# A recurrent attention and two expert layers on one core: masks moved to the Gram eviction, weights split by bit fields, r expanded on the host, another order of the instructions

## The chip, the cores and the metric

The kernel runs on one core of a Trainium2 chip. Time is the device time of one launch in microseconds (us); less is better. The core has TensorE (PE, matrix products), VectorE (DVE), ScalarE (ACT), GpSimd (POOL) and SyncE (SP), which here issues all the transfers. Each engine works through its own list of instructions in the order in which the program gives them, and an instruction waits until the semaphores that it names are set; so whatever stands behind a waiting instruction on the same engine waits too.

## The reference

Three parts follow each other. The first is a recurrence over 768 steps for 4 x 8 heads of width 40; the other two work on 3072 tokens of width 320.

```
for t in range(768):                       # state: 40x40 per head
    y[t]  = r[t] @ state
    Sa    = state @ a[t]
    state = state*w[t] - outer(Sa, b[t]) + outer(v[t], k[t])
x = y as (3072, 320)
xn = x / rms(x) * g;  x = (silu(xn@w_gate) * (xn@w_val)) @ w_out       # 64-bit weights, inner width 1536
logits = x@gate;  P = 8 rounds of row and column normalization of exp(logits)
out = sum over 8 experts of P[:,e] * (relu(x@w1[e]) @ w2[e])           # inner width 1024
```

## The kernel before, in words

**The recurrence** is cut into 24 chunks of 32 steps (c = 0 to 23), and the eight heads into three groups (s = 0, 1, 2 with 3, 3 and 2 heads). `early(c,s)` has what doesn't need the state: it loads a, b, k, v, w (`ldE`) and r (`ldr`), makes running products of w (`scan`, `rec`), scales a, b, k by them (`ag`, `bb`, `kk`), spreads r and scaled a over a block diagonal with three ACT instructions each (`rb`, `abe`), multiplies the Gram matrices on PE (`gr`) and evicts them to the tile W (`Wg`). W goes to DRAM (`stL`) and comes back in another layout, once for a batch of chunks as the input of a triangular inverse (`ldL`, `subst`), and once for each chunk and group as the tile V (`ldW`). `subst` inverts by 31 steps of a product (`mul`, L383) and a subtraction (`sub`, L384) on DVE. Its result returns through DRAM as `th`. `late2` makes from V the block diagonal `lak`, a masked copy in V (`vm`) and `kb`. `chain(c,s)` then carries the state: `Sb` (block diagonal of the state), c1 (transpose), c2, c3, c4 (with the inverse `th`), c5, the new state F and its decayed form Rn for the next chunk, and y, which is stored. So one chunk's chain starts from the chunk before it; a batch's chains wait for that batch's inverse.

**The first expert layer (moe1)** works in six blocks j of 512 tokens, and a block needs y of four chunks. `xload`, `xprep` and `xsplit` load, normalize and split x into two parts; then 12 steps f per block follow, each with two `up` groups of 8 matmuls (L596; `sig`, `sgm`, `pr`, `h`, `l` evict them) and one `down` group of 8 (L612 to L618). Its weights come as 64-bit floats. `decode(f,k)` splits each of 48 pieces into two 32-bit parts with ACT, DVE and POOL instructions (`da` to `dl`, L522 to L531) and stores them in DRAM, from where each f loads them. The three working tiles a, p, q have one buffer each, so a piece begins when the piece before has left them.

**The second layer (moe2)** runs 8 experts x 6 blocks x 8 steps: 8 matmuls up, 12 down (L712, L725 to L727). The kernel also inspects w against limits (`wx`, `wmin`, `wmax`) for a fallback path.

**The order** is not written by hand. Every piece of work is given to a planner (`Plan`) with an engine, a duration, a due time, and what it reads and writes. `order` runs a list schedule over these: on each engine, of what is ready it takes what is due first. The result is the fixed list of each engine. Due times of chunk c come from `tm` (T00, 21 us a chunk at first, then TSL = 29); decoding is due from DEC0 in steps of DECT; what is not marked `fix` takes its due time from what needs it. Until the first `up`, matmuls on zeros (`fill`, L308) are put where the plan leaves PE idle.

Of the kernel before, what the change touches and what calls it, by code (L numbers as in the profile page):

```python
# [31 lines left out]
VW=2*X2+X2  # L32
# [18 lines left out]
def host_attn(r,k,v,w,a,b,nch=NC):  # L51
# [52 lines left out]
class Plan:  # L104
# [3 lines left out]

    LAT={("ACT","PE"):.267,("P","PE"):.25,("P","ACT"):.23,("PE","ACT"):.25,("DVE","P"):.23,("PE","DVE"):.25,("ACT","DVE"):.16,
# [3 lines left out]
    def add(self,eng,dur,due,fn,reads=(),writes=(),after=(),tail=0.0,take=None,give=None,label="",fix=False,cols=None,x=None):  # L113
        self.ops.append(dict(cols=dur*2270 if cols is None else cols,eng=eng,dur=dur,due=due,fn=fn,reads=list(reads),writes=list(writes),after=list(after),
            tail=1.5+(x or 0) if eng=="SP" and x else tail,x=x,take=take,give=give,label=label,fix=fix,id=len(self.ops)))
    def lat(self,a,b): return self.LAT.get((a["eng"],b["eng"]),.2)
    def order(self,slots,free,slack=1.4,slack_sp=2.0):
# [39 lines left out]
        evq=sorted([0.0]+list(free.values()))  # L157
        while len(res)<n:
            while fut and fut[0][0]<=now+1e-9:
                r,i=heapq.heappop(fut); soon[ops[i]["eng"]].discard((r,ops[i]["due"],i)); heapq.heappush(pend[ops[i]["eng"]],(ops[i]["due"],i))  # L160
            for e,h in pend.items():
                while h and free.get(e,0.0)<=now+1e-9:
                    skipped=[]; pick=None
                    while h:
                        d,i=heapq.heappop(h)
                        t=ops[i]["take"]
                        if t and (not ring[t] or min(ring[t])[0]>now+1e-9):
                            skipped.append((d,i)); continue
# [10 lines left out]
                    end=now+o["dur"]; free[e]=end; tail=o["tail"]  # L179
                    if e=="SP" and o["x"]:  # L180
# [71 lines left out]
def attention(G_,I,xT,scrL,scrT,nch,tm,T=21):  # L252
# [66 lines left out]
    def early(c,s,due):  # L319
# [4 lines left out]
        o=spot("W",0,c)[0]; plan.place(("W",s,c),o+VW*H0[s],o+VW*(H0[s]+q))  # L324
# [23 lines left out]
        if 'A'[c%len('A')]=="D": A("DVE",dve(3*q*C),due,lambda: nc.vector.tensor_copy(*wg()),["gr"],["W"],s,c,give=("gr",s,c),label=f"Wg{c},{s}")  # L348
        else: A("ACT",act(3*q*C),due,lambda: nc.scalar.activation(out=wg()[0],in_=wg()[1],func=ACTF.Copy),["gr"],["W"],s,c,give=("gr",s,c),label=f"Wg{c},{s}")
# [12 lines left out]
    def subst(k,due,span):  # L362
# [8 lines left out]
        o=spot("TT",0,k)[0]; parts=[(0 if y=="D" else 1,a,e) for y,a,e in [["D",0,C]]]  # L371
# [3 lines left out]
        for y,(z,a,e) in enumerate(parts):  # L375
            eng,cost=(("DVE",dve),("P",pool))[z]; tn=f"tmp{y}"
            for j in range(a,C-1):
# [5 lines left out]
                A(eng,cost(r*m),dd,lambda j=j,sh=sh,t=t,V=V,x=tt[:,a:a+r]: V.tensor_tensor(t,x[:,:,j:j+1].to_broadcast(sh),lu[:,j:j+1,j+1:].to_broadcast(sh),ALU.mult),[("TT",y,k),("LU",0,k)],[kt],label=f"mul{'.abc'[y]}{k},{j}")  # L383
                A(eng,cost(r*m),dd,lambda j=j,t=t,V=V,x=tt[:,a:a+r]: V.tensor_tensor(x[:,:,j+1:],x[:,:,j+1:],t,ALU.subtract),[kt],[("TT",y,k)],label=f"sub{'.abc'[y]}{k},{j}")  # L384
# [10 lines left out]
    def late2(c,s,due):  # L395
        m=KT[s]; q=NH[s]; k=bof[c]; c0,nb=batches[k]; n=KE[s]
        V=X["V",s,c]; Vm=V[:m]
        if c>0:
# [13 lines left out]
        A("ACT",z(s,3*act(8*D),.64),due,expand,["V",("cst",)],["kb"],s,c,label=f"kb{c},{s}")  # L412
# [5 lines left out]
    def chain(c,s,due):  # L418
# [510 lines left out]
```

## Time and profile before

| | |
|---|---|
| time, median of 3 runs | 2495.6 us (2489.71 to 2497.9) |
| profiled execution: time; span from the first to the last instruction | 2487.21 us; 2485.4 us |
| busy PE; DVE; ACT; POOL | 2387.0; 1099.4; 876.6; 651.5 us |
| granted clock of TensorE, mean | 0.975 |
| HBM read; written | 183.01; 45.61 MB |
| matmuls on zeros (L308) | 1051, 138.0 us |

Busy time is the time in which at least one instruction of the engine was under way. Ends of matmuls are modelled, so a busy PE is not PE at its peak. The profile's "idle before" of an instruction is the time in which its engine stood still just before it, with what ended that.

### The profile page before, as it was taken

What the parts mean: (1) busy time and instruction counts of PE and PEld (TensorE: products, weight loads), DVE (VectorE), ACT (ScalarE), POOL (GpSimd) and SP (SyncE); (2) the same over time, 40 slices, a digit from 0 to 9 for tenths busy, and PEclk for the clock granted to TensorE, in tenths of its full rate; (3) what the DMA queues carried; (4) which work ended last, traced back from release to release, by engine and by line L of the source; (5) the groups of instructions that cost most, each with busy time, mean ns of one, the idle gap of its engine ahead of it and who ended that gap; (6) DMA issues with size and microseconds to landing.
All of it is one profiled execution on the core that took longest, in us unless ns stands there. A gap on an engine that the chain in (4) does not pass through costs nothing.

```text
span 2485.4 us, 43767 instructions
## 1 busy us (share of the span) xinstructions
PE 2387.0 (96%) x17435; PEld 2057.2 (83%) x17435; DVE 1099.4 (44%) x2169; ACT 876.6 (35%) x2079; POOL 651.5 (26%) x803
## 2 busy tenths in 40 slices
PE   8889889998999999799999999999999999999998
PEld 6777667787777877589899999988999989999887
DVE  7897996757576433621252222222222222222222
ACT  6465647565574544332221211211211211211111
POOL 5465655444453344330041100200200200100000
PEclk9998899999999999899999999999999999999999
DMA  9677678685876657740010000100100100000000
GB/s 241 185 184 159 172 208 229 163 221 152 205 192 176 177 143 215 229 126 1 11 37 1 27 21 1 46 2 1 47 1 1 47 1 10 27 1 1 11 25 31
DMA packets 263663, 231.59 MB, mean 93 GB/s; under 512 B 131801, under 2 KB 225049, under 8 KB 263449
## 3 DMA queue, kind: packets, MB, share of 16 engines
q1 hardware_dynamic: 263448, 228.70, 33.9%
q8 instruction: 139, 2.28, 0.4%
q14 instruction: 76, 0.61, 0.1%
HBM read 183.01 MB, written 45.61 MB: 92 GB/s over the span
## 4 chain that ended last, share of the span: by engine, by line
PE 74%; DVE 9%; DMA 3%; issue 1%; ACT 1%; SPq 0%; POOL 0%; DVEq 0%; ACTq 0%; POOLq 0%
PE bank L712 29%; PE bank L725 9%; PE bank L726 9%; PE bank L727 9%; PE bank L596 7%; DVE f L383 3%; DVE f L384 2%; PE bank L612 1%; PE bank L444 1%; PE bank L443 1%; PE bank L450 1%; PE bank L615 1%; PE bank L463 1%; PE bank L616 1%; PE bank L462 1%
## 5 line engine op out<-in xcount | busy, mean ns | idle before, releaser
L712 PE MATMUL bank<-r,r 128*128 128x512 f32 x3072 | 774.3, 394 | 0.0
L717 DVE SCALAR_TENSOR_TENSOR r<-bank,r 128x512 fp32r<-128x512 f32 x384 | 265.2, 691 | 893.6 <-ACT r L716 893.5
L712 PEld LDWEIGHTS bank<-r,r 128*128 128x128 f32 x3072 | 561.4, 188 | 101.5
L716 ACT ACTIVATE r<-bank 128x512 fp32r<-128x512 f32 x384 | 229.8, 599 | 1054.3 <-PE bank L712 1054.3
L725 PE MATMUL bank<-r,r 128*128 128x320 f32 x1536 | 475.4, 310 | 0.0
L726 PE MATMUL bank<-r,r 128*128 128x320 f32 x1536 | 474.2, 309 | 0.0
L727 PE MATMUL bank<-r,r 128*128 128x320 f32 x1536 | 474.1, 309 | 0.0
L705 POOL TENSOR_TENSOR r<-f,r 128x320 fp32r<-128x320 f32 (+1 forms) x128 | 120.9, 949 | 904.4 <-ACT r L704 901.9
L596 PE MATMUL bank<-r,r 128*128 128x512 f32 x1152 | 311.3, 416 | 11.7 <-ACT r L585 4.9
L726 PEld LDWEIGHTS bank<-r,r 128*128 128x128 f32 x1536 | 288.3, 188 | 17.2
L725 PEld LDWEIGHTS bank<-r,r 128*128 128x128 f32 x1536 | 288.3, 188 | 16.7 <-issue 1.0
L727 PEld LDWEIGHTS bank<-r,r 128*128 128x128 f32 x1536 | 288.3, 188 | 0.0
L596 PEld LDWEIGHTS bank<-r,r 128*128 128x128 f32 x1152 | 217.1, 196 | 62.6 <-ACT r L585 6.0
L312 ACT ACTIVATE f<-f,f 120x128 f32<-120x128 f32 (+1 forms) x568 | 183.1, 393 | 16.4 <-POOL f L337 9.5
L308 PE MATMUL bank<-f 128*128 128x256 bf16 x1051 | 138.0, 290 | 1.5 <-POOL f L298 1.5
L735 DVE SCALAR_TENSOR_TENSOR f<-bank,f,f 128x320 f32<-128x320 f32 x168 | 84.3, 544 | 112.6 <-PE bank L727 112.6
L308 PEld LDWEIGHTS <-f 128*128 128x128 bf16 x1051 | 106.7, 103 | 20.7 <-POOL f L298 1.5
L605 POOL TENSOR_TENSOR r<-f,r 128x512 fp32r<-128x512 f32 x72 | 93.7, 1301 | 109.6 <-ACT r L603 107.3
L383 DVE TENSOR_TENSOR f<-f,f 96x60 f32<-96x60 f32 (+27 forms) x248 | 113.9, 459 | 15.8 <-DMA f<-sL 11.0
L384 DVE TENSOR_TENSOR f<-f,f 96x60 f32<-96x60 f32 (+27 forms) x248 | 112.1, 452 | 4.6
L315 POOL TENSOR_TENSOR f<-f,f 120x480 f32<-120x480 f32 (+1 forms) x69 | 71.2, 1032 | 151.7 <-DVE f L470 132.0
L443 PE MATMUL bank<-f,f 96*96 96x72 f32 (+1 forms) x576 | 95.9, 251 | 2.6 <-DVE f L471 1.3
(156 smaller groups left out, 2775.1 us busy)
## 6 DMA issues: line engine op xcount, KB each, us to landing
r<-wd SPq DMA_DIRECT2D x72, 768.0 KB, 4.8
r<-wd SPq DMA_DIRECT2D x72, 320.0 KB, 3.6
sL<-f SPq DMA_DIRECT2D x96, 176.0 KB, 4.1
f<-in_pk SPq DMA_DIRECT2D x48, 301.9 KB, 4.8
wd<-r SPq DMA_DIRECT2D x48, 256.0 KB, 3.4
f<-in_w SPq DMA_DIRECT2D x64, 192.0 KB, 2.4
f<-sL SPq DMA_DIRECT2D x48, 216.0 KB, 4.3
f<-in_w SPq DMA_DIRECT2D x64, 160.0 KB, 2.3
```

What stands on the lines that cost most here:

```text
L308: def fill(): nc.tensor.matmul(G_.banks[0][:,0:256],fz[:,0:128],fz[:,128:384],start=True,stop=True)
L312: nc.scalar.activation(out=out[:,:,q,:],in_=plain,func=ACTF.Copy,scale=mbe[:KE[s],q:q+1])
L383: A(eng,cost(r*m),dd,lambda j=j,sh=sh,t=t,V=V,x=tt[:,a:a+r]: V.tensor_tensor(t,x[:,:,j:j+1].to_broadcast(sh),lu[:,j:j+1,j+1:].to_broadcast ...
L384: A(eng,cost(r*m),dd,lambda j=j,t=t,V=V,x=tt[:,a:a+r]: V.tensor_tensor(x[:,:,j+1:],x[:,:,j+1:],t,ALU.subtract),[kt],[("TT",y,k)],label=f"s ...
L596: for i,(a,k) in enumerate(PAS): PE.matmul(b,w[:,k//3,3*g+k%3],xs[:,a],start=i==0,stop=i==7)
L705: A("P",pool(n),0,lambda lo=lo,hi=hi,raw=raw: PO.tensor_tensor(lo,raw,hi,ALU.subtract),[kr,kh],[kl],label=f"wl{e},{f},{z}")
L712: for i,(a,k) in enumerate(PAS): PE.matmul(b,w[:,k],t[:,a],start=i==0,stop=i==7)
L716: A("ACT",act(TB),due+1.8,lambda: AC.activation(out=h,in_=bk[ku],func=ACTF.Relu),[ku],[kh],fix=True,label=f"R{e},{j},{f}")
L717: A("DVE",dve(TB),due+2.4,lambda: DV.scalar_tensor_tensor(l,bk[ku],0.0,h,ALU.max,ALU.subtract),[ku,kh],[kl],give=ku,fix=True,label=f"Q{e}, ...
L725: PE.matmul(p,h[:,s],w[:,0],start=f==0,stop=False)
L726: PE.matmul(p,h[:,s],w[:,1],start=False,stop=False)
L727: PE.matmul(p,l[:,s],w[:,0],start=False,stop=f==7)
```

## The change

1. The Gram matrices are masked (strictly upper triangle) when they are evicted: `Wg` is a DVE product of PSUM with the mask instead of an ACT copy. So `vm` goes, V is narrower (VW = 2*X2+D), and `lak` is three ACT copies with a scale instead of one POOL product.
2. `ag`, `bb`, `kk` go from POOL to DVE; `Sb` goes from POOL to ACT (three scaled copies).
3. r spread over the block diagonal is made on the host and loaded (`ldrb`, one transfer for each c and s, three buffers), so the ACT work `rb` goes.
4. F is written by one DVE instruction over both parts instead of two (F, Fy). In c3 of the two-head group the four products with `lak` come first, then the four with `abl`; before they alternated.
5. `decode`: the clamp of small weights (`da`, `db`) is left to the fallback. The high part is cut out of the high word by masks, the low part is put together as an integer, converted by ACT (`dg`) and multiplied by the exponent on POOL (`dl`). Per piece DVE has dc, dd, di, dq, ds (five, before six), ACT dh and dg (two, as before), POOL one (before two). `dc` and `di` now read the high words of the 64-bit pieces directly (every second word).
6. moe2 inspects the 64-bit weights too: 60 more loads, each with two DVE instructions.
7. The planner treats POOL and those DVE instructions that are marked `port` as one resource. Batches of the inverse are 1, 3, 3, 3, 3, 3, 4, 4 chunks (before 2, 3, 3, 3, 3, 3, 3, 4), and the first batch's inverse is two independent parts. Due times change (T00, DEC0, DECT, MINC; `lo` keeps decoding from becoming due earlier than its step).

```
-VW=2*X2+X2
+VW=2*X2+D
+WW=3*X2
-    for n in [2, 3, 3, 3, 3, 3, 3, 4]:
+    for n in [1, 3, 3, 3, 3, 3, 4, 4]:
...
-                        if t and (not ring[t] or min(ring[t])[0]>now+1e-9):
+                        if t and (not ring[t] or min(ring[t])[0]>now+1e-9) or ops[i]["port"] and port>now+1e-9:
...
+                    if o["port"]: port=end
...
-        rb=q5(tl("rb",n,s,c)[:,0:LP*q],q); r=X["r",s,c]
-        A("ACT",z(s,.88,.59),due,lambda: bd_act(rb,r,s),[("r",0,c),("cst",)],["rb"],s,c,label=f"rb{c},{s}")
+        rbt=tl("rb",n,s,c)[:,0:LP*q]; rb=q5(rbt,q)
+        A("SP",.5,due-T,lambda: nc.sync.dma_start(out=rbt,in_=I[f"rb{s}"][:,c]),[],["rb"],s,c,x=n*LP*q*4/360e3,label=f"ldrb{c},{s}")
-        A("P",.42,due,lambda: nc.gpsimd.tensor_tensor(ag,x(0),G4[:,:,0:C],ALU.mult),["pk","G"],["ag"],s,c,label=f"ag{c},{s}")
+        A("DVE",.2,due,lambda: nc.vector.tensor_tensor(ag,x(0),G4[:,:,0:C],ALU.mult),["pk","G"],["ag"],s,c,port=True,label=f"ag{c},{s}")
...
-        else: A("ACT",act(3*q*C),due,lambda: nc.scalar.activation(out=wg()[0],in_=wg()[1],func=ACTF.Copy),["gr"],["W"],s,c,give=("gr",s,c),label=f"Wg{c},{s}")
+        A("DVE",dve(3*q*C),due,lambda: nc.vector.tensor_tensor(*wg(),mji.unsqueeze(1).unsqueeze(1).to_broadcast([128,q,3,C]),ALU.mult),["gr",("cst",)],["W"],s,c,give=("gr",s,c),label=f"Wg{c},{s}")
...
-        A("P",z(s,.95,.68),due,lambda: nc.gpsimd.tensor_tensor(lak,Vm[:,:,D:X2].unsqueeze(2).to_broadcast([m,4,q,C]),
-            mla[:m,:q].unsqueeze(1).to_broadcast([m,4,q,C]),ALU.mult),["V",("cst",)],["lak"],s,c,label=f"lak{c},{s}")
+        def lakf():
+            for x in range(q): nc.scalar.activation(out=lak[:,:,x,:],in_=Vm[:,:,D:X2],func=ACTF.Copy,scale=mbt[:m,x:x+1])
+        A("ACT",z(s,.88,.59),due,lakf,["V",("cst",)],["lak"],s,c,label=f"lak{c},{s}")
...
-            Z("P",z(s,.95,.68),0,lambda: bd_tt(Sb,Rx[:,:,C:],s,D),["Rx"],["Sb"],"Sb")
+            Z("ACT",z(s,.98,.66),0,lambda: bd_act(Sb,Rx[:,:,C:],s),["Rx"],["Sb"],"Sb")
...
+            else:
+                for g in range(4): l(g,start=g==0,stop=False)
+                for g in range(4): h(g,start=False,stop=g==3)
...
-        A("ACT",act(n),due,lambda: AC.activation(out=Fl(a),in_=Fl(hi),func=ACTF.Abs),[kr],[ka],label="da"+z)
-        A("DVE",dv2(n),due,lambda: DV.tensor_scalar(Fl(a),Fl(a),2.0**-15,None,ALU.max),[],[ka],label="db"+z)
-        A("P",pool(n),due,lambda: PO.tensor_tensor(Fl(q),Fl(q),Fl(a),ALU.subtract),[ka],[kq],label="de"+z)
-        A("P",pool(n),due,lambda: PO.tensor_tensor(Fl(p),Fl(p),h,ALU.subtract),[kh],[kp],label="df"+z)
-        A("DVE",dve(n),due,lambda: DV.scalar_tensor_tensor(l,Fl(q),2.0**-20,Fl(p),ALU.mult,ALU.add),[kq,kp],[kl],label="dl"+z)
+        A("DVE",dv2(n),due,lambda: DV.tensor_scalar(a,src1,3,0x3ffff000,ALU.logical_shift_left,ALU.bitwise_and),[kr,ks1],[ka],port=True,lo=due,label="dc"+z)
+        A("DVE",dv2(n),due,lambda: DV.tensor_scalar(a,hi,0x1ff,15,ALU.bitwise_and,ALU.logical_shift_left),[kr],[ka],port=True,lo=due,label="di"+z)
+        A("DVE",dve(n),due,lambda: DV.scalar_tensor_tensor(q,lo,17,a,ALU.logical_shift_right,ALU.bitwise_or),[kr,ka],[kq],port=True,lo=due,label="dq"+z)
+        A("ACT",act(n),due,lambda: AC.activation(out=Fl(a),in_=q,func=ACTF.Copy,scale=2.0**-35),[kq],[ka],lo=due,label="dg"+z)
+        A("DVE",dv2(n),due,lambda: DV.tensor_scalar(p,p,-0x800000,None,ALU.bitwise_and),[kh],[kp],port=True,lo=due,label="ds"+z)
+        A("P",pool(n),due,lambda: PO.tensor_tensor(l,Fl(a),Fl(p),ALU.mult),[ka,kp],[kl],lo=due,label="dl"+z)
...
-        t=max(t,tm(4*j+4)+MLAG); dt=max(U,(tm(4*j+8)-tm(4*j+4))/12 if j<NB-1 else U)
+        t=max(t,tm(4*j+4)+MLAG+MINC*j); dt=max(U,(tm(4*j+8)-tm(4*j+4))/12 if j<NB-1 else U)
...
-DEC0,DECT=20.0,4.6; MLAG=30.0
+DEC0,DECT=-60.0,4.0; MLAG,MINC=30.0,6.0
...
-T00,TSL=70.0,29.0
+T00,TSL=55.0,29.0
```

DVE's list at the start of the program, before: one decoding piece (L523 to L531), then running products and reciprocals (L335, L336). Names like f_640_202 are areas of one big SBUF arena.

```order
L523 TENSOR_SCALAR f_320_203<-f_320_203 128x256
L524 TENSOR_SCALAR f_320_203<-f_320_203 128x256
L525 SCALAR_TENSOR_TENSOR f_320_204<-f_640_202,f_320_203 128x256
L527 TENSOR_SCALAR f_320_203<-f_320_204 128x256
L528 SCALAR_TENSOR_TENSOR f_320_205<-f_640_202,f_320_203 128x256
L335 SCALAR_TENSOR_TENSOR f_132_97<-f_644_96,f_132_89 120x132
L336 RECIPROCAL f_128_98<-f_132_97 120x128
```

The same place after the change (L343 is `scan`, L344 `rec`, L345 to L347 `ag`, `bb`, `kk`, L537 to L543 decoding, L356 `Wg`):

```order
L343 SCALAR_TENSOR_TENSOR f_132_97<-f_644_96,f_132_89 120x132
L344 RECIPROCAL f_128_98<-f_132_97 120x128
L345 TENSOR_TENSOR f_128_99<-f_644_96,f_132_97 120x128
L343 SCALAR_TENSOR_TENSOR f_132_107<-f_644_106,f_132_89 120x132
L346 TENSOR_TENSOR f_128_100<-f_644_96,f_128_98 120x128
L347 TENSOR_TENSOR f_128_101<-f_644_96,f_128_98 120x128
L537 TENSOR_SCALAR f_320_205<-f_640_204 128x256
L343 SCALAR_TENSOR_TENSOR f_132_115<-f_644_114,f_132_89 80x132
L538 SCALAR_TENSOR_TENSOR f_320_206<-f_640_204,f_320_205 128x256
L345 TENSOR_TENSOR f_128_109<-f_644_106,f_132_107 120x128
```

The first chunk's products now stand ahead of the first decoding piece, and products that POOL made are between them.

PE's list at c3 of the two-head group, before (one of 23 places; L443 is the product with `lak`, L444 that with `abl`; two of the four pairs):

```order
L443 MATMUL bank_86<-f_864_143,f_384_151 64x72
L444 MATMUL bank_86<-f_288_190,f_384_176 64x72
L443 MATMUL bank_86<-f_864_143,f_384_151 64x72
L444 MATMUL bank_86<-f_288_190,f_384_176 64x72
```

After (L448 and L449 are the same products):

```order
L448 MATMUL bank_83<-f_736_149,f_384_157 64x72 x4
L449 MATMUL bank_83<-f_288_177,f_384_174 64x72 x4
```

The eight products are the same; the change of operand shape between 64 and 80 rows happens once instead of seven times.

PE's list behind the recurrence's last c5 (L460), before: the rest of moe1's block 4 begins.

```order
L460 MATMUL bank_86<-f_864_154,f_320_164 80x72 x4
L612 MATMUL bank_79<-r_512_226,r_640_222 128x512
...
L617 MATMUL bank_81<-r_512_225,r_640_222 64x512
L596 MATMUL bank_85<-r_2560_197,r_1536_218 128x512 x8
L596 MATMUL bank_83<-r_2560_197,r_1536_218 128x512 x8
L612 MATMUL bank_79<-r_512_217,r_640_227 128x512
```

After (L472 is c5, L609 `up`, L625 to L630 `down`):

```order
L472 MATMUL bank_83<-f_736_156,f_320_166 80x72 x4
L609 MATMUL bank_85<-r_2560_199,r_1536_220 128x512 x8
L625 MATMUL bank_79<-r_512_219,r_640_224 128x512
...
L630 MATMUL bank_81<-r_512_218,r_640_224 64x512
L609 MATMUL bank_86<-r_2560_199,r_1536_225 128x512 x8
L609 MATMUL bank_84<-r_2560_199,r_1536_225 128x512 x8
```

From the last c5 to the first `up` of block 5, PE's list had 4 `up` groups and 4 `down` groups of block 4; it has 9 and 6 now.

## Rows read from the trace of the kernel before

**Rows 1.** Busy time by stretch of the whole span, chosen as the prediction says
```profile
core 0: us, PE busy (x) PEld busy (x) DVE busy (x) ACT busy (x) POOL busy (x), PEclk, DMA share, GB/s
0.00:397.50 397.50, 346.97 (x3791) 280.17 (x3791) 343.09 (x749) 218.06 (x634) 224.12 (x321) 0.91 0.75 193
397.50:975.00 577.50, 555.53 (x5553) 449.63 (x5553) 332.36 (x703) 323.52 (x849) 248.48 (x309) 0.98 0.68 182
975.00:1016.00 41.00, 22.94 (x94) 16.57 (x92) 22.46 (x30) 23.63 (x42) 28.57 (x25) 0.81 0.83 264
1016.00:1085.00 69.00, 68.68 (x292) 55.23 (x293) 33.75 (x56) 18.97 (x31) 17.60 (x14) 0.97 0.58 189
1085.00:2485.40 1400.40, 1392.91 (x7712) 1255.58 (x7710) 367.78 (x634) 292.42 (x526) 132.73 (x136) 1.00 0.06 19
```
**Rows 2.** Groups of DVE instructions, 0 to 397.5 us: busy us, mean ns | idle before
```profile
L384 DVE TENSOR_TENSOR f<-f,f 96x60 f32<-96x60 f32 (+23 forms) x124 | 59.4, 479 | 1.8
L383 DVE TENSOR_TENSOR f<-f,f 96x60 f32<-96x60 f32 (+23 forms) x124 | 53.3, 430 | 4.7 <-DMA f<-sL 3.1
L523 DVE TENSOR_SCALAR f<-f 128x256 f32<-128x256 f32 (+1 forms) x48 | 30.0, 625 | 13.9 <-ACT f L522 13.4
L531 DVE SCALAR_TENSOR_TENSOR r<-f,f 128x256 fp32r<-128x256 f32 (+1 forms) x48 | 28.0, 583 | 13.0 <-POOL f L530 12.9
L525 DVE SCALAR_TENSOR_TENSOR f<-f,f 128x256 int32<-128x256 int32 (+1 forms) x48 | 25.8, 537 | 3.0 <-DVE r L531 0.5
L524 DVE TENSOR_SCALAR f<-f 128x256 int32<-128x256 int32 (+1 forms) x48 | 22.2, 463 | 1.1
L405 DVE TENSOR_TENSOR f<-f,f 96x128 f32<-96x128 f32 (+1 forms) x14 | 6.5, 467 | 0.0
```
**Rows 3.** Timeline of DVE, first decoding piece, no POOL work beside it: start, us
```profile
4.31 0.29 DVE L524 TENSOR_SCALAR f<-f 128x256 int32<-128x256 int32 x1
4.63 0.43 DVE L525 SCALAR_TENSOR_TENSOR f<-f,f 128x256 int32<-128x256 int32 x1
```
**Rows 4.** Timeline of DVE and POOL, 792 to 800 us
```profile
792.27 0.68 DVE L601 TENSOR_TENSOR f<-bank,f 128x512 f32<-128x512 f32 x1
792.87 0.41 DVE L384 TENSOR_TENSOR f<-f,f 128x252 f32<-128x252 f32 x1
793.20 0.32 DVE L466 TENSOR_TENSOR f<-bank,f 120x160 f32<-120x160 f32 x1
797.98 1.38 DVE L383 TENSOR_TENSOR f<-f,f 128x252 f32<-128x252 f32 x1
799.73 0.28 DVE L405 TENSOR_TENSOR f<-f,f 96x128 f32<-96x128 f32 x1
797.72 1.35 POOL L605 TENSOR_TENSOR r<-f,r 128x512 fp32r<-128x512 f32 x1 [0.52 <-ACT r L603]
```
**Rows 5.** DVE busy with L384 alone, in the inverse of the last batch
```profile
779.20:813.60 34.40, 11.62 (x31) 1.00 0.60 171
```
**Rows 6.** Groups of POOL instructions, 0 to 397.5 us
```profile
L530 POOL TENSOR_TENSOR f<-f,r 128x256 f32<-128x256 f32 (+1 forms) x48 | 39.5, 822 | 43.5 <-ACT r L526 41.7 <-DMA f<-in_wm 1.0 <-DMA sL<-f 0.8
L315 POOL TENSOR_TENSOR f<-f,f 120x480 f32<-120x480 f32 (+1 forms) x23 | 23.2, 1010 | 10.5 <-DVE f L470 9.2 <-DMA f<-in_v 0.7 <-PE bank L443 0.6
L474 POOL TENSOR_TENSOR f<-f,f 120x128 f32<-120x128 f32 (+1 forms) x23 | 13.7, 596 | 0.7 <-POOL f L405 0.7
```
**Rows 7.** Group of the ACT copies onto block diagonals, 0 to 397.5 us
```profile
L312 ACT ACTIVATE f<-f,f 120x128 f32<-120x128 f32 (+1 forms) x270 | 86.6, 393 | 14.1 <-POOL f L337 9.5 <-DMA f<-in_r 3.0 <-PE bank L444 0.9
```
**Rows 8.** Timeline of PE: c3 of a three-head and of the two-head group
```profile
826.63 0.31 PE L443 MATMUL bank<-f,f 96*96 96x72 f32 x2
...
827.93 0.71 PE L612 MATMUL bank<-r,r 128*128 128x512 f32 x2
...
836.85 0.34 PE L443 MATMUL bank<-f,f 64*64 64x72 f32 x2
...
838.99 0.73 PE L612 MATMUL bank<-r,r 128*128 128x512 f32 x2
```
**Rows 9.** Timeline of PE behind the last c5, and at block 5's first up
```profile
974.94 0.72 PE L460 MATMUL bank<-f,f 128*80 128x72 f32 x8
975.47 0.71 PE L612 MATMUL bank<-r,r 128*128 128x512 f32 x2
...
977.40 3.81 PE L596 MATMUL bank<-r,r 128*128 128x512 f32 x16
981.05 0.62 PE L612 MATMUL bank<-r,r 128*128 128x512 f32 x2
...
1015.80 0.79 PE L596 MATMUL bank<-r,r 128*128 128x512 f32 x1 [1.24 <-ACT r L585]
```
**Rows 10.** Waits of PE, 975 to 1016 us: in total, times, longest
```profile
PE bank L639 <- ACT f L636: 11.2, 1, 11.2
```

More of the change, by code (lines that the diff above doesn't have):

```diff
@@ L56, in host_attn @@
     ins["r"]=np.zeros((120,nch,3,LP),np.float32)
+    for s in range(3):
+        z=np.zeros((NH[s],D,nch,B,NH[s],C),np.float32); e=em(r,s).reshape(NH[s],D,nch,B,C)
+        for q in range(NH[s]): z[q,:,:,:,q]=e[q]
+        ins[f"rb{s}"]=z.reshape(KE[s],nch,LP*NH[s])
     for s in range(3):
@@ L156, in order @@
         now=0.0; res=[]; dma=0.0; dq=[]
-        evq=sorted([0.0]+list(free.values()))
+        evq=sorted([0.0]+list(free.values())); port=0.0
         while len(res)<n:
@@ L465, in chain @@
         c5v=lambda: X["c5",s,c]
-        if c>0: Z("DVE",.235,8.8,lambda: nc.vector.tensor_tensor(F[:,:,0:D],c5v()[:,:,0:D],Rx[:,:,C:],ALU.add),["c5","Rx"],["F"],"F")
-        else: Z("ACT",.23,8.8,lambda: nc.scalar.activation(out=F[:,:,0:D],in_=c5v()[:,:,0:D],func=ACTF.Copy),["c5"],["F"],"F")
+        if c>0: Z("DVE",dve(4*X2),8.8,lambda: nc.vector.tensor_tensor(F,c5v(),Rx,ALU.add),["c5","Rx"],["F"],"F",give=("c5",s,c))
+        else: Z("ACT",act(4*X2),8.8,lambda: nc.scalar.activation(out=F,in_=c5v(),func=ACTF.Copy),["c5"],["F"],"F",give=("c5",s,c))
@@ L468, in chain @@
         if c+1<nch:
             Rn=w4(tl("Rx",n,s,c+1))
[L470 to L472 removed]
+            Z("DVE",.235,9.4,lambda: nc.vector.tensor_tensor(Rn[:,:,C:],F[:,:,C:],G[:,:,C:C+1].to_broadcast([n,4,D]),ALU.mult),["F","G"],[("Rx",s,c+1)],"Rn",port=True)
@@ L529, in decode @@
-        A("P",pool(n),due,lambda: PO.tensor_tensor(Fl(q),Fl(q),Fl(a),ALU.subtract),[ka],[kq],label="de"+z)
-        A("P",pool(n),due,lambda: PO.tensor_tensor(Fl(p),Fl(p),h,ALU.subtract),[kh],[kp],label="df"+z)
-        A("DVE",dve(n),due,lambda: DV.scalar_tensor_tensor(l,Fl(q),2.0**-20,Fl(p),ALU.mult,ALU.add),[kq,kp],[kl],label="dl"+z)
+        if not first:
+            A("ACT",act(n),due,lambda: AC.activation(out=Fl(q),in_=Fl(hi),func=ACTF.Abs),[kr],[kq],lo=due,label="da"+z)
+            A("DVE",dv2(n),due,lambda: DV.tensor_scalar(Fl(q),Fl(q),2.0**-15,None,ALU.max),[],[kq],port=True,lo=due,label="db"+z)
@@ new lines, in decode @@
+        src1,ks1=(hi,kr) if first else (q,kq)
+        A("DVE",dv2(n),due,lambda: DV.tensor_scalar(a,src1,3,0x3ffff000,ALU.logical_shift_left,ALU.bitwise_and),[kr,ks1],[ka],port=True,lo=due,label="dc"+z)
+        A("DVE",dve(n),due,lambda: DV.scalar_tensor_tensor(p,hi,-0x40000000,a,ALU.bitwise_and,ALU.bitwise_or),[kr,ka],[kp],port=True,lo=due,label="dd"+z)
+        A("ACT",act(n),due,lambda: AC.activation(out=h,in_=Fl(p),func=ACTF.Copy),[kp],[kh],lo=due,label="dh"+z)
+        A("DVE",dv2(n),due,lambda: DV.tensor_scalar(a,hi,0x1ff,15,ALU.bitwise_and,ALU.logical_shift_left),[kr],[ka],port=True,lo=due,label="di"+z)
```

96 lines of the change are left out of this document (51 added, 45 removed).

## The prediction

> **What bounds the kernel now.** I read busy time by stretch first [rows 1]. From 1085 us on PE is busy for 1392.9 of 1400.4 us at full clock, and the change leaves its work there as it is. The time is decided before. The stretches are cut at three events. At 397.5 us DVE runs the third group's step behind c4 of chunk 7; by then all 48 decoding pieces and four batches of the inverse are done. At 975 us PE starts the last c5 of the recurrence, and at 1016 us the first `up` of block 5 [rows 9], which had to wait for that c5, the store and load of y and the normalization.
>
> In the first stretch DVE is busy for 343.1 of 397.5 us, PE for 347.0 with many matmuls on zeros among them: DVE sets the pace. In the second PE is busy for 555.5 of 577.5 us: PE sets it, and recurrence and moe1 share it. [...] So there are three terms, one for each stretch.
>
> **First stretch: the balance of DVE.** I compare the work up to the same event, chunk 7's third group behind c4. The new order has there, as the old one, 9 evicted steps of moe1, 24 chain steps and four batches, and 47 pieces begun against 48.
>
> What goes from DVE: the clamp (L523, 30.0 us), the last step of decoding (L531, 28.0) and the masked copies (L405, 6.5): 64.5 us [rows 2]. F and Fy become one instruction, which I count as nothing (it saves one start and adds no columns).
>
> What comes, at durations without POOL beside them: 117 products `ag`, `bb`, `kk` at 0.28, the row of L405 with 128 columns [rows 4], 32.8 us. `di`, 46 at 0.43, 19.8 us, and `dc` 0.14 slower, 47 times, 6.6 us: both now read every second word, the nearest row that does is L525 with 0.43, while the dense L524 takes 0.29 [rows 3]. `Wg`: PSUM rows of 160 and 512 columns take 0.32 and 0.68 [rows 4], so 1.02 ns a column, 0.45 for the 288 columns of a three-head group and 0.35 for 192; 26 and 13 of them are 16.3 us. The split of the first batch adds 54 instructions but no columns; 0.41 us at 252 columns [rows 4] leaves 0.15 without the columns, 8.1 us. Together 83.6; the net is +19 us.
>
> Against that stands what POOL costs DVE. A subtraction of 252 columns takes 0.41 alone, and a product of as many 1.38 beside a POOL instruction of 1.35 [rows 4]. In this stretch L524 takes 463 ns in the mean against 290 alone, L525 537 against 430 [rows 2, 3]; over 48 each that is 8.3 and 5.1 us. The inverse takes 59.4 + 53.3 us [rows 2]; eight times the 11.62 us of a batch with little POOL [rows 5] is 93.0, so 19.7 us. That makes 33 us to get back if POOL were silent. POOL is busy for 224 us there [rows 1]; what stays are one product per piece (39.5), y (13.7) [rows 6] and some 20 us of moe1's small work: a third. So I take two thirds, -22 us, and the busy time ends at -3.
>
> DVE's idle time of 54 us has 13.9 in front of L523, waiting for ACT, and 13.0 in front of L531, waiting for POOL [rows 2]. Both instructions are gone. But the one buffer of each working tile stays: `dc` of the next piece waits for POOL's `dl`, and `ds` for ACT's `dh`. I give half of 26.9 back: -13. **The first term is -16 us.** Its ends: +41, if the products take 0.467 as L405 does in this stretch (+22), nothing of the 33 comes back and the idle time stays; -54, if strided reads cost nothing (-13), all 33 and all 27 come back (19 - 13 - 33 - 27).
>
> [...] No row here shows a one-input DVE instruction that reads with a step; I stay with 0.43.
>
> The chain hides some of this. `Sb` becomes three ACT copies of 0.39 instead of one POOL product of 1.01 [rows 6, 7]: as long, on an engine that is busy for 218 of 397.5 and 323.5 of 577.5 us [rows 1]. ACT loses `rb` and `Wg` and gains `lak` and `Sb`: 8 copies of 0.39 a chunk more, 3.1 us, less three evictions. If ACT were full, 16 chunks of this would be up to 50 us on the chain; with 44% of the second stretch idle on ACT I count nothing. The new loads add 440 KB a chunk to queues that are 0.75 busy in the first stretch and 0.68 in the second; nothing too, unless a Gram product comes to wait for them.
>
> **Second stretch: c3 of the two-head group.** From its first product to what follows it takes 838.99 - 836.85 = 2.14 us; the three-head group's, with as many products and more rows in each, 827.93 - 826.63 = 1.30 [rows 8]. What differs is that 64 and 80 rows alternate. Grouped, seven changes become one; the saving lies between nothing and 0.84 us, and I take 0.8 for the 16 chunks that are left at 397.5 us: **-13 us**.
>
> [...]
>
> **Third stretch: what is left for the gap.** PE's order has 9 `up` and 6 `down` groups of block 4 between the last c5 and block 5, where it had 4 and 4. An `up` group takes 1.83 us (two from 977.40 to 981.05), a `down` 1.93 (975.47 to 977.40) [rows 9]. 5 x 1.83 + 2 x 1.93 = 13.0 us of PE work move from in front of the last c5 into a gap with 18.1 us to spare. The additional evictions stand beside block 5's normalization on ACT and DVE, for which I take 2 us off: **-11 us**.
>
> **moe2.** The weight inspection adds 120 DVE instructions of about half a microsecond, 60 us, beside DVE's 367.8 of 1400.4 [rows 1]. It costs nothing as long as no eviction comes late behind one that waits for its load; such a wait each time, a microsecond, would be 60 us on DVE and still find 900 us idle.
>
> **Sum.** 2487.2 - 16 - 13 - 11 = 2447. The profiled execution was 8.4 us below the median of the runs, so 2455.6; I say **2455 us**. Less than 0.3% (7.5 us) can't be told from no change here.
>
> **The rivals.**
> *DVE stays contended (slower).* The planner's one port is a matter of order; on the chip the two engines still run side by side where no semaphore holds them. If the products run at L405's 0.467 and the inverse at its present 59.4 + 53.3 us, the first term is +41 and eats the other two: 2487 + 41 - 24 = 2504, 2512 as a median. It decides from +24 on. Against it: two thirds of POOL's work is gone from this stretch. 0.15.
> *Same.* The first term ends near +16 to +30 without being that bad, or PE in the second stretch waits for ACT's `Sb` and gives its gains back: 2488 to 2503. 0.11.
> *The start gives nothing.* The net +19 and the relief -22 cancel, the idle time only changes its name: 2487 - 24 = 2463, 2471 as a median, and 2478 if c3 gives half; I count 2468 to 2488. 0.15.
> *The start gives much.* Strided reads are free and decoding no longer stalls DVE: -54 - 24 gives 2409, 2418 as a median; all below 2436. 0.17.
> My forecast, 2436 to 2468, has 0.42.
>
> **How the numbers follow.** Faster holds forecast, a start that gives nothing and one that gives much: 0.74. Same 0.11, slower 0.15. The range leaves out about one in ten at each side: below 2412 and above 2506.
>
> **What would show it.** Right: the third step behind c4 of chunk 7 before 385 us; DVE's busy time to that point within 10 us of 343; subtractions of the inverse nearer to 12 than to 15 us a batch in the first batches; c3 of the two-head group at 1.3 to 1.45 us; PE idle between the last c5 and block 5 under 8 us; span from block 5's first `up` to the end unchanged. Wrong: `ag`, `bb`, `kk` above 0.4 us; DVE waiting for POOL's or ACT's part of decoding as long as now; PE waiting at the Gram products for the host's r, or at c1 for ACT.

## The result and the profile after

The changed kernel takes 2453.5 us in the median of four runs (2447.6 to 2457.55), against 2493.4 for the kernel before on the same chip: a ratio of 0.9837 with an interval of 0.9809 to 0.9865, 1.6% faster. The profiled execution took 2447.6 us with a span of 2445.8, so its span is 39.6 us shorter than that of before.

The windows answer to [rows 1]. The first cut is again the third group's step behind c4 of chunk 7, the second the last matmul of the last c5 (0.4 us behind the cut of [rows 1]; cut like this, before has 577.9 and 40.4 us), the third block 5's first `up`, the fourth 69 us behind it.

```profile
core 0: us, PE busy (x) PEld busy (x) DVE busy (x) ACT busy (x) POOL busy (x), PEclk, DMA share, GB/s
0.00:377.30 377.30, 339.52 (x3865) 281.97 (x3865) 290.62 (x866) 216.15 (x623) 78.25 (x94) 0.91 0.84 216
377.30:932.10 554.80, 528.99 (x5448) 435.24 (x5446) 334.43 (x747) 364.05 (x963) 119.95 (x116) 0.97 0.75 195
932.10:976.80 44.70, 36.55 (x145) 25.57 (x143) 31.36 (x41) 26.97 (x48) 30.83 (x26) 0.89 0.96 310
976.80:1045.80 69.00, 69.00 (x297) 56.11 (x298) 42.37 (x76) 18.52 (x30) 18.99 (x14) 0.97 0.78 246
1045.80:2445.80 1400.00, 1392.19 (x7708) 1254.85 (x7706) 393.62 (x729) 291.87 (x525) 132.68 (x136) 1.00 0.08 25
```

The 39.6 us are divided like this: 20.2 in the first stretch, 23.1 in the second, 4.3 lost again in the third, 0.6 in moe2. In the first, DVE's busy time fell by 52.5 us, but its idle time rose from 54.4 to 86.7. In the second, PE's busy time fell by 27 us and its idle time rose a little. In the third, PE does 14 us more work and idles 8.2 us instead of 18.1.

The groups of DVE up to the first cut answer to [rows 2]; the waits of DVE and of ACT there say what its idle time ended with.

```profile
L391 DVE TENSOR_TENSOR f<-f,f 32x171 f32<-32x171 f32 (+34 forms) x151 | 48.4, 331 | 0.6
L390 DVE TENSOR_TENSOR f<-f,f 32x132 f32<-32x132 f32 (+34 forms) x151 | 47.8, 326 | 2.8 <-DMA f<-sL 2.1
...
L538 DVE SCALAR_TENSOR_TENSOR f<-f,f 128x256 int32<-128x256 int32 (+1 forms) x46 | 20.4, 444 | 0.9
...
L356 DVE TENSOR_TENSOR f<-bank,f 128x288 f32<-128x288 f32 (+1 forms) x39 | 15.3, 408 | 0.8 <-PE bank L353 0.5
L537 DVE TENSOR_SCALAR f<-f 128x256 int32<-128x256 int32 (+1 forms) x47 | 15.1, 320 | 4.3 <-POOL r L544 3.4 <-DMA f<-in_wm 0.8
L540 DVE TENSOR_SCALAR f<-f 128x256 int32<-128x256 int32 (+1 forms) x46 | 14.7, 320 | 1.1
L347 DVE TENSOR_TENSOR f<-f,f 120x128 f32<-120x128 f32 (+1 forms) x39 | 14.6, 376 | 0.0
L543 DVE TENSOR_SCALAR f<-f 128x256 int32<-128x256 int32 (+1 forms) x46 | 13.5, 294 | 37.3 <-ACT r L539 37.0
L345 DVE TENSOR_TENSOR f<-f,f 120x128 f32<-120x128 f32 (+1 forms) x39 | 12.9, 332 | 0.1
L346 DVE TENSOR_TENSOR f<-f,f 120x128 f32<-120x128 f32 (+1 forms) x39 | 12.2, 312 | 0.0
```

```profile
DVE f L543 <- ACT r L539: 37.0, 26, 3.6
...
ACT r L539 <- DMA wd<-r: 35.2, 21, 3.5
```

Read the two waits as one. `ds` (L543) waits 37 us for ACT's `dh` (L539), and `dh` waits 35 us for the store of the piece before, since the two halves of a piece have one buffer. Before, DVE's waits inside decoding were 26.9 us, in front of L523 for ACT and in front of L531 for POOL [rows 2].

PE's timeline of a two-head c3 answers to [rows 8]: 833.01 - 831.73 = 1.28 us from its first product to what follows, where it was 2.14 (columns: start, us).

```profile
831.73 0.71 PE L448 MATMUL bank<-f,f 64*64 64x72 f32 x8
832.37 0.71 PE L449 MATMUL bank<-f,f 80*64 80x72 f32 x8
833.01 0.50 PE L579 MATMUL bank<-r,r 128*128 128x512 f32 x1
```

### The profile page after: what moved, and what is told of

Read it like the earlier page. It is cut to its first block, busy times and chain, and to the rows that moved or that the text cites. A ratio compares the mean times of both kernels' runs of the same rounds, so it can differ in the third digit from the quotient of the medians.

```text
span 2445.8 us, 43748 instructions
## 1 busy us (share of the span) xinstructions
PE 2366.2 (97%) x17452; PEld 2053.7 (84%) x17452; DVE 1092.4 (45%) x2457; ACT 917.6 (38%) x2188; POOL 380.7 (16%) x386
## 4 chain that ended last, share of the span: by engine, by line
PE 77%; DMA 9%; DVE 7%; SPq 3%; issue 2%; ACT 2%; POOL 0%; DVEq 0%; ACTq 0%; POOLq 0%
PE bank L725 29%; PE bank L738 9%; PE bank L740 9%; PE bank L739 9%; PE bank L609 7%; DMA wd<-r 2%; DMA f<-sL 2%; DMA f<-in_pk 1%; PE bank L462 1%; PE bank L475 1%; PE bank L474 1%; PE bank L625 1%; PE bank L448 1%; PE bank L316 1%; PE bank L449 1%
## 5 line engine op out<-in xcount | busy, mean ns | idle before, releaser
L609 PE MATMUL bank<-r,r 128*128 128x512 f32 x1152 | 305.8, 412 | 3.1 <-DVE f L356 2.4
L738 PEld LDWEIGHTS bank<-r,r 128*128 128x128 f32 x1536 | 288.3, 188 | 16.7 <-issue 1.0
L609 PEld LDWEIGHTS bank<-r,r 128*128 128x128 f32 x1152 | 216.7, 195 | 50.4 <-DVE f L356 2.6
L320 ACT ACTIVATE f<-f,f 120x128 f32<-120x128 f32 (+3 forms) x560 | 188.6, 399 | 36.8 <-DVE f L345 18.6
L618 POOL TENSOR_TENSOR r<-f,r 128x512 fp32r<-128x512 f32 x72 | 100.7, 1398 | 310.2 <-ACT r L616 272.9
L316 PE MATMUL bank<-f 128*128 128x256 bf16 x1068 | 143.4, 293 | 1.5 <-POOL f L306 1.5
L390 DVE TENSOR_TENSOR f<-f,f 96x87 f32<-96x87 f32 (+39 forms) x275 | 94.9, 350 | 20.2 <-DMA f<-sL 17.2
L391 DVE TENSOR_TENSOR f<-f,f 96x87 f32<-96x87 f32 (+39 forms) x275 | 95.8, 354 | 3.2
L462 PEld LDWEIGHTS bank<-f,f 96*96 96x96 f32 (+1 forms) x576 | 54.9, 162 | 34.6 <-ACT f L459 12.1
L448 PE MATMUL bank<-f,f 96*96 96x72 f32 (+1 forms) x576 | 81.8, 246 | 2.1 <-DMA f<-in_v 0.7
```

The source lines that it names most:

```text
L316: def fill(): nc.tensor.matmul(G_.banks[0][:,0:256],fz[:,0:128],fz[:,128:384],start=True,stop=True)
L320: nc.scalar.activation(out=out[:,:,q,:],in_=plain,func=ACTF.Copy,scale=mbe[:KE[s],q:q+1])
L448: l=lambda g,**k: nc.tensor.matmul(p[:,g,:],fl(lak[:,g]),V[:m,g,2*X2-C:2*X2+D],**k)
L609: for i,(a,k) in enumerate(PAS): PE.matmul(b,w[:,k//3,3*g+k%3],xs[:,a],start=i==0,stop=i==7)
L618: A("P",pool(TB),due+4.8,lambda: PO.tensor_tensor(l,sg,h,ALU.subtract),[k1,k3],[("l",n)],fix=True,label=f"l{n}")
L738: PE.matmul(p,h[:,s],w[:,0],start=f==0,stop=False)
```

## The experiments

Each run was timed beside the kernel before on the same chip (three chips in all, so the medians of different rows are compared by their ratios). A ratio is to the kernel before, with its interval; the last column is the difference to 0.9837, the changed kernel's own ratio, times 2493 us. With the two intervals added in squares it is known to 8 to 10 us, so -5.5, -2 and +7 can't be told from nothing, and +12 only just.

| kernel | median, us | ratio | against the changed kernel, us |
|---|---|---|---|
| changed, c3 alternating | 2467.0 | 0.9885 [0.9866, 0.9905] | +12 |
| changed, MINC 0 | 2466.8 | 0.9899 [0.9878, 0.9919] | +15.5 |
| changed, old splitting | 2468.4 | 0.9912 [0.9882, 0.9941] | +19 |
| changed, these three undone | 2496.3 | 1.0008 [0.9992, 1.0023] | +43 |
| changed, batches of before | 2449.2 | 0.9815 [0.9792, 0.9838] | -5.5 |
| changed, products on POOL | 2449.6 | 0.9830 [0.9813, 0.9847] | -2 |
| changed, no port rule | 2460.4 | 0.9865 [0.9849, 0.9881] | +7 |
| changed, both merges doubled | 2463.8 | 0.9887 [0.9857, 0.9916] | +12.5 |
| changed, two buffers, old order | 2436.4 | 0.9767 [0.9748, 0.9787] | -17.5 |
| changed, two buffers, planned | 2415.0 | 0.9688 [0.9674, 0.9703] | -37 |
| the same, products on POOL | 2429.9 | 0.9740 [0.9728, 0.9753] | -24 |
| before, two buffers, planned | 2474.6 | 0.9919 [0.9906, 0.9932] | |

The profiled execution of a kernel is one of its runs; where it lies 7 us or more from the median, the text says so.

**c3 alternating again.**

```
-            elif s<2:
+            elif s<3:
                 for g in range(4): l(g,start=True,stop=False); h(g,start=False,stop=True)
```

> The changed kernel with the two-head group's c3 alternating again, every instruction in its place. Theory (the order alone cost 0.8 us a time): c3 of that group goes back from 1.3 to about 2.1 us; the 16 of them behind chunk 7 give +13 us, the 7 before it up to +6 if PE sets the pace there by now, so +13 to +18: 2466 to 2472 us. Rival (the 2.14 us of before were a matter of what stood around it): c3 stays at 1.3 us and the time at 2453.

Measured: c3 in its timeline is back at 843.11 - 840.97 = 2.14 us, to the hundredth what it was in the kernel before, with everything around it as in the changed kernel. So the order alone costs 0.86 us.

```profile
840.97 0.34 PE L448 MATMUL bank<-f,f 64*64 64x72 f32 x2
841.23 0.34 PE L449 MATMUL bank<-f,f 80*64 80x72 f32 x2
...
843.11 0.50 PE L579 MATMUL bank<-r,r 128*128 128x512 f32 x1
```

The two stretches of this kernel:

```profile
0.00:386.60 386.60, 349.81 (x3865) 288.46 (x3865) 289.91 (x866) 216.10 (x623) 78.05 (x94) 0.88 0.82 211
386.60:943.20 556.60, 539.16 (x5447) 440.43 (x5446) 335.84 (x747) 364.23 (x963) 119.36 (x116) 0.98 0.75 195
```

PE's busy time rose by 10 us in each; 9.3 of it show as time in the first stretch, but only 1.8 in the second, where PE's idle time fell from 25.8 to 17.4. The time, 2467.0 us, is what was expected. Where in the kernel it arises can't be told from this execution, which was 8 us below its median: seven c3 lie before the cut, 6 us, but PE's busy time there rose by 10.3, at a granted clock of 0.88 instead of 0.91, and the kernel without the port rule, which has the new c3, also has 0.88 there and its cut at 386.0 us. In the two kernels below that have the old splitting, with the old c3 and without it, the first stretches differ by only 2.7 us (408.4 and 405.7; the former also has MINC 0, which alone moves the cut by 0.4).

The cost shows with 64 and 80 rows, not with any two row counts: the three-head group alternates 96 and 120 rows in the changed kernel too, and takes 822.81 - 821.50 = 1.31 us for as many products, near the 1.28 of the grouped 64 and 80 rows. No run has its products grouped.

```profile
821.50 0.31 PE L448 MATMUL bank<-f,f 96*96 96x72 f32 x2
821.65 0.33 PE L449 MATMUL bank<-f,f 120*96 120x72 f32 x2
...
822.81 2.09 PE L609 MATMUL bank<-r,r 128*128 128x512 f32 x8
```

**MINC 0.** One number, `MLAG,MINC=30.0,6.0` to `30.0,0.0`.

> The changed kernel with MINC 0: between the last c5 and block 5 PE has 4 up and 4 down groups of block 4 again, as before the change, where the changed kernel has 9 and 6. Theory (work moved into a gap that PE waits in anyway): the last c5 comes some 13 us later, the gap to block 5 is 2 to 4 us shorter and has some 10 us more of idle PE; the end comes 9 to 11 us later, 2462 to 2465 us. Rival (the gap is stretched by what is put into it, or block 4 takes its time elsewhere): no change, 2450 to 2457.

Measured: the last c5 comes 17.0 us later (949.1 against 932.1) and the gap behind it is 0.5 us shorter, with 20.1 us of idle PE instead of 8.2.

```profile
949.10:993.30 44.20, 24.10 (x89) 16.34 (x87) 23.80 (x34) 24.89 (x45) 29.33 (x25) 0.78 0.79 249
```

```profile
PE bank L652 <- ACT f L649: 12.5, 1, 12.5
```

The 12.5 us of one wait are those of [rows 10], which the changed kernel fills with block 4. The gap is as long without the moved work as with it, where it was expected to be 2 to 4 us shorter: the work costs nothing there that shows.

**The old splitting of the weights.** The old instructions `da` to `dl` in the changed kernel, with its due times and its port rule; this also moves the order.

> The changed kernel with the splitting of the 64-bit weights of before: a clamp and a last step more on DVE, one POOL product more for each of 48 pieces, one strided step less. Theory (the fall of DVE's busy time by 52 us in the first stretch comes mostly from here, and a third of it is worth time): DVE's busy time there rises by 35 to 50 us, the event at chunk 7 comes 10 to 18 us later; 2464 to 2472 us. Rival (the new splitting traded a wait for POOL for a longer wait for the store, so its pace is the same): the event moves by less than 6 us, 2448 to 2460.

```profile
0.00:405.70 405.70, 364.20 (x4114) 305.45 (x4115) 323.00 (x929) 218.78 (x629) 123.36 (x141) 0.92 0.78 204
```

Measured: DVE's busy time to the first cut is 32 us longer, its idle time 4 us shorter, so the cut comes 28 us later, more than the whole gain there and more than the 10 to 18 that were expected; PE has 249 more instructions before it, and the second stretch is 10 us shorter. The net, 18.6 us, agrees with the time, which is in the expected range. The new splitting is the first stretch's gain.

**The three together.**

> The changed kernel with three parts undone together: the old splitting of the weights, c3 of the two-head group alternating, MINC 0. What is left of the change are the masks at the eviction, the products on DVE, the host's r, the batches, the port and the due times. Theory (three parts carry the whole gain, one for each place, and add up): 2453.5 + 18 + 13 + 15 is about 2500, so as before the change or up to 10 us slower, 2488 to 2505. Rival (they overlap, or the rest of the change gives something of its own): 2465 to 2483.

Measured: 2496.3 us, no difference to before. One by one they are worth 12 + 15.5 + 19 = 46.5 us, together 43. What is left of the change (masks, products, r from the host, batches, port, due times) adds up to nothing that these runs can tell. It does move time: with the three undone the cut comes at 408.4 us, 11 us later than before the change, and the second stretch is 11 us shorter (566.9 against 577.9).

**The batches of before.** The list `[1, 3, 3, 3, 3, 3, 4, 4]` to `[2, 3, 3, 3, 3, 3, 3, 4]`.

> The changed kernel with the batches of before, 2, 3, 3, 3, 3, 3, 3 and 4 chunks, the first one still in two column parts. Theory (the first stretch gained by DVE's balance): the first inverse begins some 18 us later, as before the change, but chunk 7 only 0 to 6 us; time 2453 to 2460 us. Rival (the gain of 20 us in the first stretch is the head start that a first batch of one chunk gives, 31.8 against 50.1 us for its first product): chunk 7 comes 12 to 20 us later and the time is 2465 to 2473.

Measured: the first inverse begins at 48.7 us instead of 31.8, and chunk 7's step comes at 374.7 instead of 377.3. A head start of 17 us is used up before chunk 7. The rival, for which the head start is the gain, fell; event and time lie a few us below the theory's ranges, which is within the noise (the profiled execution was 9 us above its median).

**The products on POOL.** `nc.vector` to `nc.gpsimd` for `ag`, `bb`, `kk`, with the planner's price of before.

> The changed kernel with the products ag, bb and kk on POOL again, as before the change; the planner moves other work around them. Theory (DVE's time in the first stretch is part work, part contention with POOL, and a third of what is added to DVE appears as time, as the doubled merges showed with 13 of 42 us): DVE loses 40 us of products and gets 10 to 20 back as longer instructions of the inverse and of decoding; the event at chunk 7 moves by less than 8 us either way; 2446 to 2461. Rival (contention weighs more than the work, DVE and POOL hold each other's semaphores): the event comes 10 to 20 us later and the Gram products wait for POOL again; 2464 to 2474.

Measured: no difference in the medians. In its profiled execution, which was 7 us above its own median, the first cut came 12 us later and the second stretch was 3 us shorter; the cut is thus between the theory (under 8 us) and the rival. DVE's busy time before the cut fell by only 10.3 us, though 39.7 us of products had left it. In the time the placement is neutral, as in the batches' case.

**No port rule.** The condition on `port` is taken out of `order`.

> The changed kernel with the planner's rule for the shared port left out: instructions of DVE and POOL that use it may be planned side by side, all instructions are the same. Theory (with POOL's work down to a third there is little left to keep apart): within 8 us of the changed kernel, 2446 to 2461, DVE's busy time in the first stretch up by 0 to 15 us. Rival (the rule is what made DVE's instructions shorter): DVE's busy time up by 25 us or more, 2463 to 2475.

Measured: 7 us slower, with intervals that overlap; DVE's busy time to the first cut is 297.5 us against 290.6. The rule is worth little, if anything.

**Both merges doubled.** `dd` and `dq` are issued twice in a row.

> The changed kernel with the two merges of each decoding piece issued twice in a row on DVE, same results and same order: 92 more instructions of 0.44 us, 40 us of DVE, up to the third step behind c4 of chunk 7. Theory (DVE's work sets the pace there): the event comes 30 to 40 us later, time 2483 to 2493 us. Rival (85 us of DVE's 374 are idle now and take it in): less than 10 us later, 2453 to 2463.

```profile
0.00:390.40 390.40, 341.19 (x3865) 280.11 (x3865) 332.94 (x957) 215.50 (x623) 78.16 (x94) 0.90 0.81 209
```

Measured: between the two theories. DVE has 42.3 us more to do and the cut comes 13.1 us later, a price of a third; DVE's wait at L543 falls from 37.0 to 17.9 us. (This execution was 13.5 us below the kernel's median, so the third is rough.) So work that is added where a piece waits for the store anyway is mostly hidden.

**Two buffers for a decoded piece.** First (the upper of the two new lines) the planner still sees one buffer, so that all engines keep their order; then (the lower) it knows of both.

```
-        oh=ob+3*DP; kh=put(("dh",i),oh,DP); kl=put(("dl",i),oh+DP,DP)
+        oh=ob+3*DP; kh=put(("dh",i),oh,DP); kl=put(("dl",i),oh+DP,DP); oh+=2*DP*(i%2)
+        oh=ob+3*DP+2*DP*(i%2); kh=put(("dh",i),oh,DP); kl=put(("dl",i),oh+DP,DP)
```

> The changed kernel with two buffers for a decoded piece, so that ACT's first half of a piece needn't wait for the store of the piece before; the order of all engines is the same. Theory (the first stretch is paced by DVE, whose longest wait is now for this copy on ACT, 37 us up to the third step behind c4 of chunk 7): the wait goes to under 10 us and the event comes 15 to 35 us earlier, time 2420 to 2440 us. Rival (the pace of the start is set by the chain through the inverse and the loads, and DVE's waits fall into its slack): the wait goes all the same, the event moves by less than 8 us and the time stays at 2446 to 2456.

> The changed kernel with two buffers for a decoded piece, this time known to the planner, so that the order changes with it. Theory (the wait for the store paced decoding; the planner puts the instructions of decoding closer once it needn't hold them): as the two buffers in the old order, 2436 us, or up to 10 us below. Rival (the tighter order of decoding delays the chain on DVE): 2440 to 2450.

The waits of L543 to the first cut, in the old order and in the new, then the first stretch in the old order and the first two in the new:

```profile
DVE f L543 <- ACT r L539: 16.7, 14, 3.3
```

```profile
DVE f L543 <- ACT r L539: 5.4, 7, 1.8
```

```profile
0.00:367.30 367.30, 330.30 (x3865) 276.52 (x3865) 287.23 (x865) 214.61 (x623) 86.08 (x94) 0.92 0.86 221
```

```profile
0.00:351.70 351.70, 321.17 (x3696) 268.12 (x3697) 281.88 (x873) 214.72 (x625) 87.60 (x94) 0.89 0.89 232
351.70:894.70 543.00, 522.59 (x5445) 431.79 (x5444) 329.06 (x739) 363.10 (x963) 119.40 (x116) 0.98 0.76 199
```

Measured: in the old order the cut comes at 367.3, 10 us earlier, and the time falls by 17.5 us. The time is in the theory's range, but the event moved less than its 15 us and the wait fell to 16.7 rather than under 10. When the planner knows, the cut comes at 351.7 and the time falls by 37 us, 11 more than the theory's best; at 2415.0 us this is the fastest kernel of the study, 3.1% below the one before, for a buffer whose room was reserved and unused.

**The same, with the products on POOL.**

> The changed kernel with two buffers for a decoded piece, known to the planner, and with the products ag, bb and kk on POOL. Theory (with the wait for the store gone DVE's work sets the pace at the start again, so 40 us less of it are worth more than the third that they were): 5 to 15 us below the same kernel with the products on DVE, 2400 to 2410 us. Rival (PE and the loads pace it by now, or what POOL takes of DVE's time eats it): 2411 to 2422.

```profile
0.00:349.90 349.90, 315.41 (x3669) 262.99 (x3670) 265.47 (x747) 213.82 (x622) 125.63 (x210) 0.89 0.87 228
349.90:914.40 564.50, 533.56 (x5443) 439.71 (x5442) 313.71 (x649) 362.86 (x965) 164.07 (x216) 0.96 0.75 195
```

Both theories fell. DVE is 16 us less busy at the start, which is worth 1.8 us, and the second stretch is 21.5 us longer than with the products on DVE (543.0), half of it PE's busy time and half its idle time. PE's waits there name the chain's ACT instructions (L475 for L465 and L462 for L459: 19.6 us, 7.6 with the products on DVE), but what makes them late was not isolated.

**Two buffers in the kernel before.** The planned edit of above.

> The kernel before with two buffers for a decoded piece, known to the planner. Theory (before the change the first stretch was paced by DVE's work and not by the store of a decoded piece, which no DVE wait names there): the event at chunk 7 moves by less than 8 us, time 2485 to 2497 us. Rival (the single buffer paced decoding before the change too): 15 to 35 us earlier, 2458 to 2478.

```profile
0.00:378.20 378.20, 327.08 (x3492) 261.96 (x3493) 328.83 (x748) 214.18 (x628) 241.77 (x319) 0.85 0.78 202
```

The theory fell. The cut comes 19 us earlier (378.2 against 397.5), as much as by the whole change, with 14 us less busy time on DVE and 5 us less idle time; the time falls by 0.8%, some 20 us. So the single buffer, with the order that the planner made for it, held up the start before the change as well. Which of the two did it is open here: no run has the second buffer in the old order of this kernel.

## Why the prediction was right, and where it was not

The sum was right, 2455 against 2453.5, and each of the three terms was near: the start -16 (measured -20.2 to the cut), c3 -13 (-12 by undoing it), the tail -11 (-15.5 by undoing it). That one part stands behind each term is shown by undoing all three, which gives the time of before. Behind the first number, though, stand two errors that cancelled: that it came near is luck.

**First stretch, DVE's ledger: too dark by far.** I had DVE's busy time at -3 us; it fell by 52.5. Of the groups that I had priced, the products came at 39.7 us (32.8) and `Wg` at 15.3 (16.3). `di` took 14.7 instead of 19.8, and `dc` fell from 22.2 us [rows 2] to 15.1, where I had let it rise by 6.6 less its part of the relief. DVE's timeline of the first pieces has both alone:

```profile
7.76 0.29 DVE L537 TENSOR_SCALAR f<-f 128x256 int32<-128x256 int32 x1 [0.79 <-DMA f<-in_wm]
...
8.83 0.28 DVE L540 TENSOR_SCALAR f<-f 128x256 int32<-128x256 int32 x1
```

A one-input instruction that reads every second word takes the 0.29 of the dense one [rows 3]. My row for it, L525, was a two-input merge, and that was what its 0.43 told, not the step: the old last step of decoding, a two-input merge of dense words, takes as long when it is alone, as the run with the old splitting shows.

```profile
14.70 0.42 DVE L541 SCALAR_TENSOR_TENSOR r<-f,f 128x256 fp32r<-128x256 f32 x1
```

The inverse fell from 112.7 to 96.2 us with 54 instructions more, where I had -5. POOL's busy time fell from 224 to 78 us. That POOL's work lengthens these instructions agrees with the runs in which the products move to POOL: its busy time rises from 78.3 to 132.7 us with one buffer and from 87.6 to 125.6 with two, and the same 302 instructions of the inverse take 100.7 us instead of 96.2 and 101.4 instead of 95.1. But my own rows give 93.0 + 8.1 = 101.1 us with POOL silent, so the row for a batch [rows 5] or the price of the split was too high as well. Scan, smaller groups and records that overlap make up the rest, which I didn't split.

**First stretch, the idle time: the wrong sign.** I gave half of 26.9 us back. That DVE would wait for `dh` was named in the prediction, but it was priced as a remainder of the old waits, not as a wait of its own behind the store: 37.0 us, and all of DVE's idle time rose by 32. The profile of before had this wait two steps behind the one that I dropped: DVE's L531 waited for POOL's L530, POOL's L530 waited 41.7 us for ACT's L526 [rows 6], and ACT's L526 waited for the store.

```profile
ACT f L522 <- POOL f L529: 60.3, 29, 5.5
ACT r L526 <- DMA wd<-r: 21.7, 18, 3.4
```

Taking L531 away took away the last link and not what held it. That DVE waits for ACT's part of decoding as long as before was one of the signs listed as "wrong", and it came, without making the time wrong.

**"DVE sets the pace" was the step that failed.** A share of 86% was read as the bound. With two buffers in the kernel before, DVE's share hardly changes (328.8 of 378.2 us, 87%) and the stretch is 19 us shorter. DVE's work is nearly the same: the durations of its instructions there add up to 374.1 us, before to 376.9. The busy time fell by 14 us because more of them overlap, the idle time by 5. So DVE was busy and yet held up, by the round of load, split, store through one buffer or by the order made for it. In the changed kernel the buffer alone, in the same order, moves the cut by 10 us, and 42 us more DVE work cost only 13. The old splitting cost 28 at the cut for 32 us of DVE's. The difference between these two prices fits a chain: the old splitting has one POOL instruction and one DVE step more between a piece's load and its store, while the doubled merges stand partly where ACT waits. The products on POOL, which stand outside that chain, gained nothing by leaving DVE, with one buffer or with two. That it is this chain is argued from these runs; none of them lengthened it without adding work to DVE or POOL.

**Second term.** The size per chunk was right: the order alone costs 0.86 us (2.14 against 1.28), where I had 0.8. What PE does in that time these runs don't show. The place stays open: the run with c3 alternating has most of the difference in the first stretch, which I had given to DVE alone, and little in the second, but at different clocks.

**Third term.** The mechanism was right: work moved into the gap costs nothing there. It was mis-sized by the 2 us taken off for evictions beside the normalization, which the gap doesn't show (44.2 us without the moved work, 44.7 with it), and the windows have 14.2 us moved rather than 13.0. PE's idle time there is 8.2 us where I had said under 8. That the gap is 4 us longer than before has another cause in the change, since it stays with MINC 0; which one is open.

**moe2** was right: from block 5's first `up` to the end 1469.0 us against 1469.6. The two new groups of DVE there are 44.3 us (60 estimated); they wait 18 us for their loads, and PE is busy for 1392.2 of 1400.0 us as before.

```profile
L801 DVE TENSOR_REDUCE f<-f 128x1 f32<-128x256 f32 (+1 forms) x60 | 22.5, 377 | 1.5
L800 DVE TENSOR_SCALAR f<-f 128x256 int32<-128x256 int32 (+1 forms) x60 | 21.8, 367 | 18.1 <-DMA f<-in_wm 17.9
```

Of the rivals, the contended DVE needed `ag`, `bb`, `kk` at 0.467 us (they take 0.31 to 0.38) and an unchanged inverse. The rival in which the start gives nothing had the idle time that only changes its name, but not the fall of the busy time. The rival in which the start gives much had the cost of the strided reads right; its other condition, that decoding no longer stalls DVE, did not come, and only the two buffers brought it.

## What to carry to other kernels

A busy share of 86% doesn't prove a bound: follow the idle 14% to what ends it, and on through the engines that it waits for; if that ends with a store that frees the only buffer, count that round first. A second buffer, with the order that the planner made for it, gave 0.8% to the old kernel and 1.5% to the new one. When a wait's instruction is removed, ask which wait of the same chain comes to light, rather than giving a part of it back. Look in the trace whether alternating shapes cost time: 64 and 80 rows did (2.14 us alternating, 1.28 grouped), while 96 and 120 took 1.31 us alternating. Work that can run in a known gap should be ordered into it. The c3 order and the gap were both priced to within 5 us from rows of the old profile, though these runs know each only to 8 to 10 us.

## What the runs showed of the hardware that was not expected

A DVE instruction with one input ran as fast over every second 32-bit word as over dense ones (256 columns: L537 and L540 0.29 and 0.28 us, the dense L524 of before 0.29). Eight small products that alternate between 64 and 80 rows took 2.14 us, 0.86 more than grouped ones, while eight that alternate between 96 and 120 rows took 1.31. And the spread of a kernel's runs can go with the granted clock of TensorE: of six executions of the kernel with the doubled merges the shortest span is 2448.4 us at a mean clock of 0.977, the longest 2476.1 at 0.966. So a difference of a few us between single profiled executions, stretch by stretch, says little.
